# First-layer pieces of two pairs' tails moved later, with a new order and new loads, in a fused windowed-attention and MLP-mixer kernel

## The chip, the cores and the metric

The kernel runs on one core of one Trainium2 chip. The metric is the device time of one execution, in microseconds (us). A core has a matrix engine (PE, with its weight loads shown as PEld), a vector engine (DVE), a scalar engine (ACT), GpSimd (POOL) and SyncE (SP), and DMA engines that move data beside them. POOL and SP do little arithmetic here: POOL issues the loads from memory and some stores, SP issues transposing DMAs (from one on-chip buffer to another) and the other stores.

## What is computed

Eight images of 576 tokens. First, attention over a causal window of 128 tokens, 8 heads of 64 values, with a linear bias per head; then a mixer block with one matrix product pair over tokens and one over channels.

```python
scores = scale * np.matmul(q, k.transpose(0, 1, 3, 2))     # q, k, v: 8 x 8 x 576 x 64
bias = slopes[:, None, None] * (-np.abs(rel))[None, :, :]
mask = (rel >= 0) & (rel < 128)
attn = softmax(np.where(mask, scores + bias[None], -1e9))
x = (attn @ v) as 8 x 576 x 512
h = np.maximum(xt @ w_tok1, 0.0) @ w_tok2                  # over tokens: 576 -> 256 -> 576
u = x + h.transpose(0, 2, 1)
h2 = np.maximum(u @ w_ch1, 0.0) @ w_ch2                    # over channels: 512 -> 1536 -> 512
return u + h2
```

## The kernel before

**Tiling.** An image has 576 tokens: four blocks of 128, called main tokens here, and a tail of 64. Two images (`b` even and odd) form a pair (`pr`); their two tails make one block of 128 rows, `TAIL`, number 8 of the pair's nine blocks. All matrix work is in bf16 with 128 x 128 weights.

**Stages of one image.** `side(b)` does attention and the token mixer: the loaded `qk` blocks are turned (`transposes`; on PE through `ident`, line 679, for the first ten blocks of the run, later by a transposing DMA that SP issues, line 668, from `qk` to `qkT`), then `scores` (PE line 722, exponential on ACT, mask on DVE), `values` (PE line 802, divided into `xb`), then `token_mix` (PE lines 847, 857, 889 and, for the tail, 885), whose result `ub` (tail: `utl`) is turned again by DMA from image 2 on (line 915) into `uT` (tail: `uTt`). `main(b)` does the channel mixer: the first layer writes `r2` (tail: `r2t`), the second layer (`second`, PE line 1326; tail: `tail_second`, PE line 1218) writes the output. While `main(b)` runs, `side(b + 1)` is woven in between.

**The first layer and its pieces.** For the main tokens it consists of twelve chunks (`chunk`, PE line 1085, four matmuls of 512 columns each) or, for a number of images set by `UNITS`, of units (`unit`, PE line 1006) that use seven half-size products instead of eight. `UNITS = [0,0,0,1,2,1,2,3]`: image 3 has one unit and image 7 three. In `main`, images with units run through `for u in range(NHT // 4)`, that is u = 0, 1, 2.

**The tails.** The tails of images 0 to 3 go through the channel mixer together in `main(3)`, those of images 4 to 7 in `main(7)`. The first layer of such a group of tails is done by `tail_piece(t)`: each call makes two pieces of eight matmuls of 256 columns (PE line 1129), each followed by a ReLU on ACT (line 1134) into `r2t`. Three calls, t = 3, 7 and 11, cover the twelve tiles. The pieces read `uTt`, of which the transposing DMA of the group's later pair is the last part.

**What sets the order.** Nothing above runs in the order written. Every call of `plan.op` records an operation with an engine, a cost, a rank (its due time) and its dependences; `Plan.run` then deals the operations out, engine by engine: of those that can start, the one with the smallest start and then the smallest rank. `along` hands out ranks: each operation gets the sum of the costs of those before it in its stage, so the place where a call stands in `main` sets its rank and that of what comes behind it. `SEEDS` shifts the rank of each group of 30 operations within a stage by a pseudo-random amount of up to `SHIFT` = 1500 either way. Loads are the exception: POOL issues them strictly in the order in which they were recorded, for the first pair and the weights that of `LOADS` (`k2` is k of block 2, `W` the token weights, `A` and `B` quarters of the channel weights, `P` and `T` small parts for the tails). Where PE is planned to wait within the first part of the run, `Plan.emit` fills the gap with matmuls on zeros (`spin`, PE line 1418), sized by the gap.

Of the kernel before, what the change touches and what calls it, by code (L numbers as in the profile page):

```python
# [73 lines left out]
class Plan:  # L74
# [235 lines left out]
    def emit(self, spin):  # L310
# [11 lines left out]
        for _, _, go in sorted(work, key=lambda w: w[:2]):  # L322
# [20 lines left out]
RANKH = 0  # L343
RELU = 350
SUMS_AT = 60e3
SEEDS = {0: 517497, 4: 785877, 5: 700536, 6: 16714, 7: 413526, 8: 685397, 10: 382165, 11: 797072, 20: 274424, 21: 252221, 22: 938434, 23: 229954, 30: 618980, 31: 73962, 40: 48116, 41: 463500, 42: 138947, 50: 698411, 60: 77721, 61: 670382, 62: 980070, 70: 272112, 71: 329646, 73: 863296, 80: 860821, 81: 812390, 82: 698755, 90: 642555, 91: 36162, 92: 820492, 100: 378208, 101: 12283, 102: 666882, 110: 374839, 111: 457165, 112: 228977, 122: 958618, 130: 444343, 131: 112543, 132: 417601, 140: 895813, 141: 108506, 142: 904489, 151: 79725, 152: 698131, 153: 848768, 154: 58892}
GROUP = 30
SHIFT = 1500.0
UNIT_LATE = False
# [28 lines left out]
EARLY = 1  # L378


LOADS = ("k2 k8 q2 k1 q1 v3 v0 v1 v8 q8 v2 q7 W1 q5 q6 k6 k7 "
         "W2 v7 v6 k5 A1 q4 A0 k4 B0 A2 v4 A3 B3 B2 v5 P1 T0 B1")


@with_exitstack
def kernel(
# [81 lines left out]
    W1 = const.tile([P, NC, DTOK], BF16, name="W1")  # L468
    W1p = const.tile([P, 2, DTOK], BF16, name="W1p")
    W2 = const.tile([P, NJ, NC * P], BF16, name="W2")  # L470
# [585 lines left out]
    def main(b, rank):  # L1056
# [64 lines left out]
        def tail_piece(t):  # L1121
            uTt = tails_of(pr)[1]
            for w in (t - 3, t - 1):
                cx = bank()

                def gox(w=w, cx=cx):
                    for i in range(2):
                        for cb in range(NCB):
                            pe_.matmul(cx()[:, 2 * i * P : 2 * (i + 1) * P], lhsT=WC1[:, cb, (w + i) * P : (w + i + 1) * P],  # L1129
                                       rhs=uTt()[:, cb, :], start=cb == 0, stop=cb == NCB - 1)  # L1130

                rk = rank(872)
                plan.op("PE", 872, gox, rk, makes=cx, reads=[(uTt, 0), (uTt, 1)], needs=[lc1[w], lc1[w + 1]])
                plan.op("ACT", 600, lambda w=w, cx=cx: act_.activation(
                    out=r2t()[:, w : w + 2, :], in_=cx().rearrange("p (a b) -> p a b", a=2), func=ACT.Relu),
                    rk, part=(r2t, w // 2), uses=[cx], other=("DVE", 690, lambda w=w, cx=cx: dve_.tensor_scalar(
                        out=r2t()[:, w : w + 2, :], in0=cx().rearrange("p (a b) -> p a b", a=2), scalar1=0.0,
                        scalar2=None, op0=ALU.max)))

        if not UNITS[b]:  # L1140
            turn_ = [0, 1, 2, 6, 7, 8, 3, 4, 5, 9, 10, 11] if quick else list(range(NHT))
            for at, t in enumerate(turn_):
                rk = chunk(t)
                if quick and at % 6 == 5:
                    second_sums(at // 6, rk)
                if late_tail and at % 4 == 3:
                    tail_piece(at)
        else:
            tt = halves(b, rank, uT)
            for u in range(NHT // 4):  # L1150
                if u >= NHT // 4 - UNITS[b]:
                    rk = unit(b, u, rank, uT, tt, r2)
                else:
                    for t in (2 * u, 2 * u + 1, 6 + 2 * u, 7 + 2 * u):
                        rk = chunk(t)
                if quick and u:
                    second_sums(u - 1, rk)
                if late_tail:
                    tail_piece(4 * u + 3)
        if late_tail and TAIL_FIRST[pr // 2]:  # L1160
            tail_second(b, rank, r2t)
        second(b, rank, r2, ss, sums, ub)
# [291 lines left out]
```

## Time and profile before

| | us |
|---|---|
| runs | 274.56, 274.52, 273.83 (median 274.52) |
| the profiled execution's own time | 275.12 |
| its span, first to last instruction | 273.4 |
| PE busy | 267.6 |
| DVE busy | 230.4 |
| ACT busy | 148.9 |
| POOL busy (issuing) | 112.9 |

The profile is one execution. Its span leaves out 1.72 us around the program. A busy PE does not mean that PE is at its peak, since a matmul's end is modelled and overlaps the next; how long a stretch took is better read from the starts.

### The profile page before, as it was taken

What the parts mean: (1) busy time and instruction counts of PE and PEld (TensorE: products, weight loads), DVE (VectorE), ACT (ScalarE), POOL (GpSimd) and SP (SyncE); (2) the same over time, 40 slices, a digit from 0 to 9 for tenths busy, and PEclk for the clock granted to TensorE, in tenths of its full rate; (3) what the DMA queues carried; (4) which work ended last, traced back from release to release, by engine and by line L of the source; (5) the groups of instructions that cost most, each with busy time, mean ns of one, the idle gap of its engine ahead of it and who ended that gap; (6) DMA issues with size and microseconds to landing.
All of it is one profiled execution on the core that took longest, in us unless ns stands there. A gap on an engine that the chain in (4) does not pass through costs nothing.

```text
span 273.4 us, 7106 instructions
## 1 busy us (share of the span) xinstructions
PE 267.6 (98%) x2839; PEld 190.0 (69%) x2839; DVE 230.4 (84%) x543; ACT 148.9 (54%) x258; POOL 112.9 (41%) x142
## 2 busy tenths in 40 slices
PE   8999999999999999989999999999999999999994
PEld 4675667575568556765778868586578676888884
DVE  6577799998989499855999979998898899968984
ACT  5384895356931683038951079615960596047720
POOL 8999645950770077500890007800940300040000
PEclk9999999999999999999999999999999999999999
DMA  8999999999998999999999989999996800541016
GB/s 155 154 163 174 192 199 178 153 142 236 148 146 107 179 191 119 141 166 227 116 118 155 223 172 81 139 132 210 178 155 109 217 2 0 79 134 42 1 41 192
DMA packets 167553, 38.71 MB, mean 142 GB/s; under 512 B 155872, under 2 KB 166496, under 8 KB 167520
## 3 DMA queue, kind: packets, MB, share of 16 engines
q0 software_dynamic: 113936, 19.51, 91.7%
q1 hardware_dynamic: 51360, 18.10, 36.2%
q10 hardware_dynamic: 2224, 0.66, 1.2%
q8 instruction: 22, 0.36, 0.6%
q14 instruction: 11, 0.09, 0.1%
HBM read 35.85 MB, written 9.44 MB: 166 GB/s over the span
## 4 chain that ended last, share of the span: by engine, by line
PE 94%; DMA 3%; DVE 1%; issue 0%; DVEq 0%
PE ps L1326 25%; PE ps L1085 19%; PE ps L1006 10%; PE ps L802 7%; PE ps L722 7%; PE ps L847 5%; PE ps L889 4%; PE ps L1418 4%; PE ps L1129 4%; PE ps L1218 3%; DMA uTt<-utl 3%; PE ps L679 2%; PE ps L857 1%; PE ps L885 1%; PE ps L1070 1%; PE ps L924 1%
## 5 line engine op out<-in xcount | busy, mean ns | idle before, releaser
L535 POOL DMA_DIRECT2D v<-in_v_dram x40 | 34.5, 867 | 85.8 <-PE ps L802 84.0
L757 ACT ACTIVATE pe<-ps 128x1024 bf16<-128x1024 f32 (+1 forms) x62 | 56.0, 956 | 19.7 <-PE ps L722 19.5
L1085 PE MATMUL ps<-uT,WC 128*128 128x512 bf16 x232 | 55.4, 380 | 0.0
L1326 PEld LDWEIGHTS <-r 128*128 128x128 bf16 x372 | 35.8, 98 | 6.3 <-issue 0.8
L1091 ACT ACTIVATE r<-ps 128x512 bf16<-128x512 f32 x51 | 29.9, 599 | 18.4 <-PE ps L1085 18.1
L1085 PEld LDWEIGHTS <-WC 128*128 128x128 bf16 x232 | 21.1, 97 | 20.8
L535 POOL DMA_DIRECT2D qk<-in_q_dram x38 | 33.0, 878 | 2.8 <-DMA v<-in_v_dram 2.6
L535 POOL DMA_DIRECT2D qk<-in_k_dram x38 | 33.3, 890 | 1.4 <-DMA WC<-in_moe_w_ch_dram 1.0
L767 DVE TENSOR_TENSOR pe<-pe,mask 128x1024 bf16<-128x1024 bf16 (+1 forms) x50 | 32.4, 664 | 0.9 <-ACT pe L757 0.8
L1326 PEld LDWEIGHTS <-s 128*128 128x128 bf16 x288 | 27.6, 98 | 4.8 <-issue 0.5
L818 DVE TENSOR_TENSOR xb<-ps,rt 128x256 bf16<-128x256 f32 (+1 forms) x68 | 27.3, 416 | 0.7
L802 PEld LDWEIGHTS <-pe 128*128 128x128 bf16 (+1 forms) x560 | 22.4, 98 | 6.1 <-DVE pe L767 1.2
L802 PE MATMUL ps<-v,pe 128*128 128x65 bf16 (+1 forms) x560 | 26.1, 194 | 0.0
L1326 PE MATMUL ps<-WC,r 128*128 128x256 bf16 x192 | 24.4, 273 | 0.0
L1326 PE MATMUL ps<-WT,s 128*128 128x256 bf16 x192 | 23.9, 273 | 0.0
L1326 PE MATMUL ps<-WT,r 128*128 128x256 bf16 x180 | 22.1, 273 | 0.0
L722 PEld LDWEIGHTS <-qkT 64*128 64x128 bf16 x560 | 14.8, 94 | 10.5 <-issue 8.5
L744 ACT ACTIVATE pe<-ps 128x1024 bf16<-128x1024 f32 x7 | 7.2, 1022 | 26.1 <-PE ps L722 26.1
L907 DVE TENSOR_TENSOR ub<-ps,xb 128x512 bf16<-128x512 f32 x30 | 19.0, 683 | 0.8 <-PE ps L889 0.8
L722 PE MATMUL ps<-qkT 64*128 64x128 bf16 (+1 forms) x304 | 19.3, 216 | 0.1
L815 DVE RECIPROCAL rt<-ps 128x4 f32<-128x4 f32 (+1 forms) x76 | 12.6, 176 | 6.0 <-PE ps L802 5.1
L847 PE MATMUL ps<-xb,W 128*128 128x512 bf16 x64 | 16.4, 379 | 0.0
(118 smaller groups left out, 459.4 us busy)
## 6 DMA issues: line engine op xcount, KB each, us to landing
v<-in_v_dram POOLq DMA_DIRECT2D x32, 128.0 KB, 5.3
qk<-in_k_dram POOLq DMA_DIRECT2D x30, 128.0 KB, 5.4
qk<-in_q_dram POOLq DMA_DIRECT2D x30, 128.0 KB, 5.3
WC<-in_moe_w_ch_dram POOLq DMA_DIRECT2D x8, 384.0 KB, 10.0
out_dram<-raw SPq DMA_DIRECT2D x10, 256.0 KB, 2.5
out_dram<-raw SPq DMA_DIRECT2D x18, 128.0 KB, 3.1
out_dram<-ob SPq DMA_DIRECT2D x7, 256.0 KB, 2.5
out_dram<-raw POOLq DMA_DIRECT2D x5, 256.0 KB, 2.6
```

The costliest lines, as they stand in the source:

```text
L535: nc.gpsimd.dma_start(out=to()[p0 : p0 + n, :, :], in_=rows(src, b, s0, n))
L722: pe_.matmul(wide(e)[:, i, 0 if joint else kind, a:z], lhsT=ts[kb]()[e * D : (e + 1) * D, NHP + i, :], rhs=ts[blk]()[e * D : (e + 1) * D, ...
L757: act_.activation(out=pb()[:, e, :, lo:, c0:c1_], in_=wide(e)[:, :, lo:, c0:c1_], func=ACT.Exp, scale=scale)
L767: dve_.tensor_tensor(out=o, in0=o, in1=heads(mk, es), op=ALU.mult)
L802: pe_.matmul(view()[a:z, at, i, :], lhsT=pb()[:, e, i, kind, a:z], rhs=vb()[:, h, 0 : D + 1], start=m == 0, stop=m == len(mms) - 1, skip_g ...
L818: dve_.tensor_tensor(out=x4(), in0=view()[r0:r1_, :, :, 0:D], in1=rt()[r0:r1_, 0:n, :, :].broadcast_to([r1_ - r0, n, 4, D]), op=ALU.mult)
L847: pe_.matmul(t1[j]()[:, :], lhsT=W1[:, c, j * P : (j + 1) * P], rhs=xb()[:, blk, :], start=c == 0, stop=False)
L907: plan.op("DVE", 690, lambda blk=blk, u=u_of(pr, blk)[1], ht=ht, hs=hs: dve_.tensor_tensor(out=u(), in0=ht()[:, hs], in1=xb()[:, blk, :], ...
L1006: pe_.matmul(bk()[:, c * HS : (c + 1) * HS], lhsT=l(c, cb), rhs=r(cb), start=new and c == 0 and cb == 0, stop=cb == 1, skip_group_check=True)
L1085: pe_.matmul(ct()[:, :], lhsT=WC1[:, cb, t * P : (t + 1) * P], rhs=uT()[:, cb, :], start=cb == 0, stop=cb == NCB - 1)
L1091: plan.op("ACT", 600, lambda t=t, ct=ct: act_.activation(out=r2()[:, t, :], in_=ct()[:, :], func=ACT.Relu), rk, part=(r2, t), uses=[ct], o ...
L1326: pe_.matmul(of(bk, c), lhsT=l(t, c), rhs=w(t), start=first, stop=g == 1 and t == HK - 1, skip_group_check=True)
```

## The change

Three things are different, and no arithmetic is.

1. The place of the tail pieces among the main tokens' pieces. Images 3 and 7 both take the path with units. There, `tail_piece(3)`, `(7)` and `(11)` stood behind u = 0, 1 and 2; now nothing stands behind u = 0, `tail_piece(3)` behind u = 1, and `(7)` and `(11)` behind u = 2. The same shift is made in the path without units, which no image with a late tail takes.
2. `SEEDS`, the table that shifts ranks: 47 groups with a number before, 44 now, nearly all with another number.
3. `LOADS`, the order of the first pair's loads and the weights: the same 35 items in another order.

```diff
...
-SEEDS = {0: 517497, 4: 785877, 5: 700536, 6: 16714, 7: 413526, 8: 685397, 10: 382165, 11: 797072, 20: 274424, 21: 252221, 22: 938434, 23: 229954, 30: 618980, 31: 73962, 40: 48116, 41: 463500, 42: 138947, 50: 698411, 60: 77721, 61: 670382, 62: 980070, 70: 272112, 71: 329646, 73: 863296, 80: 860821, 81: 812390, 82: 698755, 90: 642555, 91: 36162, 92: 820492, 100: 378208, 101: 12283, 102: 666882, 110: 374839, 111: 457165, 112: 228977, 122: 958618, 130: 444343, 131: 112543, 132: 417601, 140: 895813, 141: 108506, 142: 904489, 151: 79725, 152: 698131, 153: 848768, 154: 58892}
+SEEDS = {0: 184261, 4: 385444, 6: 691587, 7: 435935, 8: 971243, 10: 14454, 11: 310335, 12: 88060, 20: 451034, 21: 604284, 22: 491458, 23: 654259, 31: 69562, 40: 313502, 41: 516766, 42: 615956, 50: 545906, 51: 396156, 60: 899926, 62: 898557, 70: 192676, 71: 113139, 72: 650006, 73: 567960, 81: 119321, 90: 576549, 92: 820979, 100: 378208, 101: 47453, 102: 655405, 111: 103762, 112: 7071, 121: 349157, 122: 783724, 130: 503198, 132: 893694, 140: 133189, 141: 34590, 142: 311199, 150: 776541, 151: 75250, 152: 65067, 153: 406410, 154: 132943}
...
-LOADS = ("k2 k8 q2 k1 q1 v3 v0 v1 v8 q8 v2 q7 W1 q5 q6 k6 k7 "
-         "W2 v7 v6 k5 A1 q4 A0 k4 B0 A2 v4 A3 B3 B2 v5 P1 T0 B1")
+LOADS = ("k1 k2 q2 q8 v8 q1 k8 v1 v0 W2 k6 v2 v3 W1 k5 q7 q4 "
+         "k7 q5 k4 q6 A0 A2 v7 A3 A1 B2 P1 v4 T0 B0 B1 v6 v5 B3")
...
-                if late_tail and at % 4 == 3:
-                    tail_piece(at)
+                if late_tail and at in (6, 9, 11):
+                    tail_piece({6: 3, 9: 7, 11: 11}[at])
...
-                if late_tail:
-                    tail_piece(4 * u + 3)
+                for t in ([], [3], [7, 11])[u] if late_tail else []:
+                    tail_piece(t)
...
```

How the order comes out is shown at three places. The first is the queue of SP where the tails of images 0 to 3 are turned (`uTt`; `ub1` and `utl0` hold image 3's token-mixer results, `qkT` is turned q and k). Before:

```order
L668 DMA_TRANSPOSE qkT2_79<-qk2_69 128x8x128
L915 DMA_TRANSPOSE uTt0_102<-utl0_95 128x4x128
L915 DMA_TRANSPOSE uT1_101<-ub1_94 128x4x128 x4
L668 DMA_TRANSPOSE qkT1_78<-qk1_68 128x8x128
L1306 DMA out_0_dram<-raw1_107 128x2x256
```

Now:

```order
L668 DMA_TRANSPOSE qkT2_79<-qk3_70 128x8x128
L915 DMA_TRANSPOSE uT1_101<-ub1_94 128x4x128
L915 DMA_TRANSPOSE uTt0_102<-utl0_95 128x4x128
L915 DMA_TRANSPOSE uT1_101<-ub1_94 128x4x128 x3
L668 DMA_TRANSPOSE qkT3_80<-qk2_69 128x8x128
```

One of the four transposing DMAs of image 3's main tokens now stands ahead of that of the tails.

The second is ACT in the same stretch, where every first-layer piece is evicted once, the tails' as line 1134, chunks of main tokens as line 1091 (lines 744 and 757 are the exponentials of scores). Before:

```order
L865 ACTIVATE r110_99<-ps_66 128x512
L744 ACTIVATE pe1_86<-ps_66 128x8x128
L1134 ACTIVATE r2t0_105<-ps_66 128x512 x2
L1091 ACTIVATE r21_104<-ps_66 128x512 x3
L757 ACTIVATE pe0_85<-ps_66 128x1024 x2
L1091 ACTIVATE r21_104<-ps_66 128x512 x2
L757 ACTIVATE pe2_87<-ps_66 128x1024 x2
L1091 ACTIVATE r21_104<-ps_66 128x512 x2
L757 ACTIVATE pe1_86<-ps_66 128x1024 x2
L1134 ACTIVATE r2t0_105<-ps_66 128x512 x2
```

Now:

```order
L1091 ACTIVATE r20_103<-ps_66 128x512
L744 ACTIVATE pe2_87<-ps_66 128x8x128
L1134 ACTIVATE r2t0_105<-ps_66 128x512
L1091 ACTIVATE r21_104<-ps_66 128x512 x2
L757 ACTIVATE pe1_86<-ps_66 128x1024 x2
L1091 ACTIVATE r21_104<-ps_66 128x512 x2
L757 ACTIVATE pe0_85<-ps_66 128x1024 x2
L1091 ACTIVATE r21_104<-ps_66 128x512 x2
L757 ACTIVATE pe2_87<-ps_66 128x1024 x2
L1091 ACTIVATE r21_104<-ps_66 128x512
L1134 ACTIVATE r2t0_105<-ps_66 128x512
```

Of the tails' six pieces in image 3, the second now stands behind seven chunks more, beside the next side's scores (line 757).

The third is POOL, whose loads follow `LOADS`; from the token weights `W1` on (a `qk` buffer takes q and k of one block). Before:

```order
L539 DMA W1_118<-in_moe_w_tok1_dram 128x4x256
L539 DMA W1p_119<-in_moe_w_tok1_dram 64x256
L535 DMA qk4_71<-in_q_dram 128x8x64
L535 DMA qk0_67<-in_q_dram 128x8x64
L535 DMA qk0_67<-in_k_dram 128x8x64
L535 DMA qk3_70<-in_k_dram 128x8x64
L539 DMA W2_120<-in_moe_w_tok2_dram 128x2x512
L535 DMA v1_73<-in_v_dram 128x8x64
L535 DMA v2_74<-in_v_dram 128x8x64
```

Now:

```order
L539 DMA W1_118<-in_moe_w_tok1_dram 128x4x256
L539 DMA W1p_119<-in_moe_w_tok1_dram 64x256
L535 DMA qk4_71<-in_k_dram 128x8x64
L535 DMA qk1_68<-in_q_dram 128x8x64
L535 DMA qk0_67<-in_q_dram 128x8x64
L535 DMA qk1_68<-in_k_dram 128x8x64
L535 DMA qk4_71<-in_q_dram 128x8x64
L535 DMA qk0_67<-in_k_dram 128x8x64
```

Before, PE turned blocks 7 and 6 first of these (`qk3` and `qk0`), complete with the sixth row here. Now it turns blocks 7 and 5 (`qk1` and `qk4`), complete with the sixth and the seventh; `W2`, seventh before, is issued ahead of this stretch now.

## The prediction

> **What bounds the kernel now.** I read the busy times first, then the same times by stage, then what PE waited for, then the chain of waits around the longest wait. In the rows by stage, each engine's busy time is followed by its instructions.
>
> ```profile
> PE 267.6 (98%) x2839; PEld 190.0 (69%) x2839; DVE 230.4 (84%) x543; ACT 148.9 (54%) x258; POOL 112.9 (41%) x142
> ...
> PE   8999999999999999989999999999999999999994
> ...
> PEclk9999999999999999999999999999999999999999
> ...
> 0.00:31.00 31.00, 29.60 (x333) 18.52 (x334) 21.53 (x68) 17.74 (x31) 28.27 (x40) 1.00 1.84 164
> 31.00:117.00 86.00, 85.99 (x916) 55.62 (x915) 75.75 (x177) 47.67 (x81) 44.56 (x54) 1.00 1.71 163
> 117.00:119.00 2.00, 1.08 (x16) 0.76 (x14) 0.82 (x2) 1.02 (x1) 0.00 (x0) 1.00 1.70 74
> 119.00:240.00 121.00, 121.00 (x1304) 88.45 (x1302) 107.52 (x238) 67.68 (x108) 37.62 (x46) 1.00 1.15 138
> 240.00:273.40 33.40, 29.90 (x280) 26.62 (x277) 24.82 (x60) 14.82 (x38) 2.48 (x4) 0.99 0.26 83
> ```
>
> PE is busy 267.6 of 273.4 us at full clock. By stage it is busy 85.99 of 86.00 us from 31 to 117 us and 121.00 of 121.00 us from 119 to 240 us. Only the first 31 us, 2 us in the middle and the last 3.5 us (stores) hold idle time. So the time is PE's own work, plus fillers and waits at the start, plus one wait at 117 us, and an order can gain no more than these.
>
> ```profile
> PE ps L1129 <- DMA uTt<-utl: 0.9, 1, 0.9
> PE ps L924 <- DVE ub L907: 0.3, 1, 0.3
> ...
> 109.05 1.42 PE ps L1326 x12
> 110.47 0.60 PE ps L885 x4
> ...
> 111.09 0.69 DVE utl L907
> ...
> 111.81 6.84 DMA uTt<-utl
> ...
> 118.69 1.03 PE ps L1129 x8
> 119.72 1.31 PE ps L1326 x12
> 121.03 0.24 PE ps L802 x8
> ```
>
> The waits on PE (total us, times, longest) behind its first instruction are two: 0.9 us for the tails' transposing DMA, 0.3 us for `ub` in the start. The chain of waits (start us, us, what) shows the first: the tail's token mixing ends at 110.47 + 0.60 = 111.07, DVE adds until 111.78, the DMA is issued at 111.81 and takes 6.84 us, and PE starts the first tail piece, line 1129, at 118.69.
>
> **What the wait costs.** The idle row is not the whole price, as matmuls overlap.
>
> ```profile
> 117.38 0.40 PE L722 MATMUL ps<-qkT 64*128 64x128 bf16 x8
> 118.69 1.03 PE L1129 MATMUL ps<-uTt,WC 128*128 128x256 bf16 x8 [0.92 <-DMA uTt<-utl]
> ...
> 90.76 1.89 PE L1085 MATMUL ps<-uT,WC 128*128 128x512 bf16 x8
> 92.66 0.23 PE L722 MATMUL ps<-qkT 64*128 64x128 bf16 x2
> ...
> 93.21 1.04 PE L1085 MATMUL ps<-uT,WC 128*128 128x512 bf16 x4
> ```
>
> Sixteen matmuls of line 722 take 0.55 us from first to next start (92.66 to 93.21). One switch of PE between tile shapes (64 rows to 128) is in that: line 1326 x12 took 1.42 us where another shape follows it, and 1.31 where none does, so a switch is 0.11 us, and eight matmuls with a switch take (0.55 - 0.11)/2 + 0.11 = 0.33. From 117.38 PE could have gone on at 117.71 instead of 118.69. The wait costs **0.98 us**.
>
> **The change, part by part.** The matmuls of the real work are the same in number and shape: all 2788. What differs is where they stand, the fillers, the switches and the waits.
>
> *The tail's first piece in image 3.* Between line 885 and the first line 1129, the order of before holds 8 matmuls of line 889, 42 of line 1326 and 8 of line 722; now 4, 60, 8 and also 8 of line 802.
>
> ```profile
> 106.35 1.29 PE ps L847 x6
> ...
> 111.81 1.19 SPq L915 DMA_TRANSPOSE uTt<-utl  x1
> 113.10 5.83 SPq L915 DMA_TRANSPOSE uT<-ub  x4
> ...
> 111.40 1.45 POOL L535 DMA_DIRECT2D qk<-in_k_dram  x2
> ...
> L915 SPq DMA_TRANSPOSE uTt<-utl x3: 1190/1216/1216, 111.8 to 236.0; - x3
> ...
> DMA to landing us min/median/max: 2.4/2.9/6.8
> ```
>
> Line 1326 costs 1.31/12 = 0.109 us each, line 889 has the shape of line 847 (1.29/6 = 0.215), eight of line 802 take 0.24. So PE has 18 x 0.109 - 4 x 0.215 + 0.24 = 1.34 us more to do first. The DMA came 118.65 - 111.07 = 7.58 us after line 885; PE was ready after 7.62 - 0.98 = 6.64, and now after 7.98. Against that, `uTt` now stands second in SP's queue behind one `uT`, and SP takes 113.10 - 111.81 = 1.29 us from one issue to the next. The block of that `uT` is finished two of line 889 and line 885 itself ahead of the tail's, 0.43 + 0.60 = 1.03 us, so `uTt` is issued 0.26 us later: 7.84. POOL's loads, which were still being issued until 112.85 (111.40 + 1.45), are freed by values at the same distance ahead of line 885 as before, so they lie on the DMA as they did. The margin is 0.14 us. The ends are -0.98 (gone) and +0.26 (the later issue, were the 1.34 us of work eaten elsewhere). I take **-0.9**, near the end of the counted rows.
>
> A rule weighed here: the row says 2.4, 2.9 and 6.8 us to landing for the three `uTt` DMAs. The Trainium skill (DMA: Bandwidth & Descriptors, Anatomy of one DMA) gives, fitted for DMAs that GpSimd issues, 2.0 us plus bytes/436e3; for 128 KB that is an estimate of 2.3 us. The trace agrees for two, not for the one at 111.81, beside POOL's loads. By the rule the DMA would not be what PE waited for, and this term would be 0, not -0.9; that is a rival below.
>
> *Pieces moved on.* The second piece of image 3 goes behind seven chunks, and the last one stays 1.75 us of PE work (12 + 4 matmuls) ahead of `tail_second` in both kernels. Their ReLUs on ACT move with them. ACT is busy 148.9 of 273.4 us, and that covers it: 0. In image 7 the first piece comes earlier: 8 of line 889, 4 of line 1006 (the shape of line 1326) and 30 of line 1326 behind line 885, 1.73 + 34 x 0.109 = 5.4 us.
>
> ```profile
> 236.02 1.22 SPq L915 DMA_TRANSPOSE uTt<-utl  x1
> ```
>
> There `uTt` stood behind two `uT`; now it is first. With utl 0.9 us behind line 885 and 2.4 to 2.9 us to landing it is there after 3.8: no wait, 1.6 us to spare.
>
> *Fillers.* 51 with 21,800 columns before, 52 with 22,704 now, all before image 0's first layer.
>
> ```profile
> 14.81 1.47 PE L1418 MATMUL ps<-zero 128*128 128x512 bf16 x6
> 16.21 0.23 PE L722 MATMUL ps<-qkT 64*128 64x128 bf16 x2
> ```
>
> Six of 512 columns ran from 14.81 to 16.21, less a switch of 0.11: 0.42 ns a column. 904 more cost **+0.38 us**, unless what they cover arrives earlier than the filler ends; they can't be negative.
>
> *Switches.* PE changes shape 98 times before, 96 times now: -2 x 0.11 = **-0.2**.
>
> *Loads.* All loads are issued as before, in another order, the same sum on POOL. At the block turned second by line 679, after the first token mixing, the order is tightest.
>
> ```profile
> 24.10 1.07 PE L679 MATMUL ps<-ident,qk 128*128 128x128 bf16 x16
> 25.00 0.60 PE L889 MATMUL ps<-r,W 128*128 128x512 bf16 x2
> ...
> 17.06 1.87 POOL L535 DMA_DIRECT2D qk<-in_k_dram  x2
> ...
> 19.49 1.92 POOL L535 DMA_DIRECT2D v<-in_v_dram  x2
> ...
> DMA to landing us min/median/max: 4.7/5.9/11.6
> ...
> L535 POOL DMA_DIRECT2D v<-in_v_dram x40 | 34.5, 867 | 85.8 <-PE ps L802 84.0 <-DMA WC<-in_moe_w_ch_dram 1.0 <-DMA qk<-in_k_dram 0.4
> ```
>
> Before, the blocks turned there, 7 and 6, were complete with k7, issued as the second of the two k loads at 17.06 (about 18), and PE came at 24.10. Now the second block is 5 and needs q5, two DMAs on, the place of the first v load at 19.49. PE comes there later by the block ahead of it, (25.00 - 24.10)/2 = 0.45 us, and by about 0.6 us of fillers and what they pushed back: 25.15. With 4.7 to 5.9 us to landing (minimum and median of the early v loads) q5 is there at 24.2 to 25.4. The wait is 0 to 0.3; a slot missed costs 0.87 us, the price of one load on POOL. I take **+0.2**, ends 0 and +0.87. The old wait of 0.3 us for `ub` (line 924) has its cause gone, as the block that came last there now goes to ACT instead of DVE, with 20 matmuls of line 679's kind, 1.1 us, ahead of its use: **-0.3**, ends -0.3 and +0.3 (DVE late again).
>
> *Scores behind the transposes of image 2.* SP issues four `uT`, then the first `qkT` of the next side.
>
> ```profile
> 82.56 5.12 SPq L915 DMA_TRANSPOSE uT<-ub  x4
> 87.78 2.63 SPq L668 DMA_TRANSPOSE qkT<-qk  x2
> ...
> qkT<-qk SPq DMA_TRANSPOSE x26, 3.9
> ```
>
> Before, PE reached that `qkT` (line 722, at 92.66) almost as it landed: eight chunk matmuls at 0.215 from 90.76 and a switch end at 92.59, so it waited 0.07 us. Now there are 66 of line 1326, 8 chunk matmuls and 4 of line 802 between, not 60, 12 and 8: 6 x 0.109 - 4 x 0.215 - 0.12 = 0.33 us less. If the DMA, 4.8 us from 87.78, is as slow again, PE waits 0.40; if it is as quick as the 3.9 us of its kind's median, not at all. I take **+0.3**, ends 0 and +0.4.
>
> **The sum.** -0.9 + 0.38 - 0.2 + 0.2 - 0.3 + 0.3 = -0.5 us. The profiled execution took 275.12, so it would take 274.6; it lies 0.6 above the median of the runs, so against the median: **274.0 us**. A difference below 0.3% (0.82 us) is about what a measurement of this kernel can't tell from none. What is late next: after 119 us nothing on PE waited, and behind 150 us the two orders are within 0.1 us of PE work of one another, so no new wait is counted there.
>
> **The rivals.**
>
> *All at the good ends.* The wait goes, the `qkT` DMA is quick, q5 is there: -0.98 + 0.38 - 0.2 - 0.3 = -1.1, 273.4 us. For it: PE has no other wait to lose. Against it: three tight places must all hold. Chance 0.24.
>
> *The wait isn't the DMA's length, or the second place in the queue eats the shift.* Then the term is 0 and the sum +0.4, 274.9 us; the change would not do what its first part is about. For it: the margin of 0.14 us. Against it: 6.84 us in the chain. Chance 0.12.
>
> *Slower: the first 30 us lose load slots.* `W2` and two v blocks now come ahead of blocks that PE turns; each slot missed at line 679 or 847 is 0.87 us for the whole of PE, which has no slack later to make it good. From two slots on it decides: -0.5 - 0.2 + 1.74 = +1.0, 275.5 us; three give 276.4. For it: the DMA engines are the limit there and the place has 0 to 0.3 us. Against it: the slots were counted by rows. Other waits that no row of before shows would look alike. Chance 0.24.
>
> **How the numbers follow.** The forecast has 0.40, with its own range 273.4 to 274.7 (the wait kept to a third, the `qkT` and q5 terms at either end). Faster by over 0.3%, below 273.7: the good ends 0.24 and 0.10 of the forecast's, 0.34. Slower, above 275.34: the load slots' 0.24 less a little under the bound, and a little of the second rival, 0.24. Between: 0.42. The range for 8 in 10 is 273.0 to 275.9, from the good ends to the middle of the slower case.
>
> **What would show it.** Right: in the waits on PE, no row for `uTt` at line 1129, or one of up to 0.3; line 1418 at 52 instructions; PE idle in the first 31 us like the 1.4 us here. The `qkT` step: a PEld row for line 722 and a DMA of 0.3 to 0.5 near 92 us. Wrong: PE's first line 1085 or 1070 later than about 31 us (the slots), a `uTt` row of about 0.9 (the second rival), or PE idle between 120 and 240 us, which nothing here foresees.

## Result and profile after

The changed kernel takes **274.97 us** (median of 11 executions, 274.27 to 275.47), the kernel before 274.35 (273.83 to 274.63): a ratio of 1.0029, 95% interval 1.0021 to 1.0038. It is slower by 0.6 us where 0.5 less was forecast. The time lies inside the range given.

Busy times of the changed kernel's profiled execution (275.40 us):

```profile
span 273.3 us, 7116 instructions
...
PE 267.4 (98%) x2840; PEld 190.2 (70%) x2840; DVE 229.4 (84%) x542; ACT 148.4 (54%) x256; POOL 113.0 (41%) x142
```

The same by stage, with the columns as in the prediction:

```profile
0.00:31.00 31.00, 28.78 (x320) 17.98 (x320) 20.96 (x64) 15.25 (x28) 27.39 (x39) 1.00 1.81 164
31.00:117.00 86.00, 86.00 (x930) 55.24 (x927) 74.94 (x181) 50.56 (x82) 45.39 (x55) 1.00 1.79 166
117.00:119.00 2.00, 2.00 (x27) 1.82 (x25) 1.63 (x3) 0.00 (x0) 0.00 (x0) 1.00 0.66 55
119.00:240.00 121.00, 121.00 (x1298) 88.73 (x1296) 106.55 (x237) 68.53 (x110) 38.05 (x46) 1.00 1.13 136
```

The wait at 117 us is gone (2.00 of 2.00 busy). The first 31 us have lost: 28.78 busy in place of 29.60. The waits on PE (total us, times, longest) say where:

```profile
PE ps L679 <- DMA qk<-in_k_dram: 0.8, 1, 0.8
PE ps L679 <- DMA qk<-in_q_dram: 0.3, 1, 0.3
```

PE's timeline shows the place (start us, us, what, in brackets the idle time ahead of it):

```profile
24.70 0.40 PE L679 MATMUL ps<-ident,qk 128*128 128x128 bf16 x4
25.90 0.40 PE L679 MATMUL ps<-ident,qk 128*128 128x128 bf16 x4 [0.80 <-DMA qk<-in_k_dram]
26.60 0.62 PE L679 MATMUL ps<-ident,qk 128*128 128x128 bf16 x8 [0.31 <-DMA qk<-in_q_dram]
```

PE turns blocks 7 and 5 there, and k7, then q5, come too late. From start to start the two waits cost 0.97 and 0.48 us beyond the matmuls' own time. The chain of waits tells the same. Until 26.6 us it runs along POOL's issues of loads, and only then along PE (first rows and the change-over):

```profile
1.37 6.87 DMA qk<-in_k_dram
8.53 0.69 POOL qk L535
...
17.57 2.29 POOL qk L535 x3
20.18 6.38 DMA qk<-in_q_dram
26.60 0.62 PE ps L679 x8
27.23 0.86 PE ps L889 x4
```

That shows a start bound by loads, but not why the kernel is slower: the waits that are gone, 0.98 us at 117 us and 0.45 us for `ub` at line 924 (both from start to start), were worth as much as the two new ones, 1.45 us. In the two profiled executions PE's last matmul even starts earlier in the changed kernel (269.37 us) than before (269.68). So either these two executions aren't typical, or the loss lies behind that matmul, and the experiments begin with that.

### The profile page after: what moved, and what is told of

The parts are those of the page before. It is cut to its first block, busy times and chain, and to the rows that moved or that the text cites. A ratio compares the mean times of both kernels' runs of the same rounds, so it can differ in the third digit from the quotient of the medians.

```text
span 273.3 us, 7116 instructions
## 1 busy us (share of the span) xinstructions
PE 267.4 (98%) x2840; PEld 190.2 (70%) x2840; DVE 229.4 (84%) x542; ACT 148.4 (54%) x256; POOL 113.0 (41%) x142
## 4 chain that ended last, share of the span: by engine, by line
PE 88%; DMA 5%; POOL 4%; issue 1%; DVE 1%; DVEq 0%; POOLq 0%
PE ps L1326 26%; PE ps L1085 19%; PE ps L1006 10%; PE ps L802 6%; PE ps L722 6%; PE ps L889 5%; PE ps L847 5%; PE ps L1129 4%; PE ps L1218 3%; DMA qk<-in_k_dram 3%; DMA qk<-in_q_dram 2%; POOL qk L535 2%; PE ps L857 1%; POOL v L535 1%; PE ps L885 1%
## 5 line engine op out<-in xcount | busy, mean ns | idle before, releaser
L1085 PE MATMUL ps<-uT,WC 128*128 128x512 bf16 x232 | 56.0, 379 | 0.0
L802 PE MATMUL ps<-v,pe 128*128 128x65 bf16 (+1 forms) x560 | 25.3, 194 | 0.0
L1326 PE MATMUL ps<-WC,r 128*128 128x256 bf16 x192 | 25.1, 273 | 0.0
L1326 PE MATMUL ps<-WT,s 128*128 128x256 bf16 x192 | 24.6, 273 | 0.0
L815 DVE RECIPROCAL rt<-ps 128x4 f32<-128x4 f32 (+1 forms) x76 | 11.7, 173 | 6.8 <-PE ps L802 6.3
L1306 POOL DMA_DIRECT2D out_dram<-raw x5 | 3.6, 714 | 33.2 <-issue 21.8
```

The source lines that it names most:

```text
L802: pe_.matmul(view()[a:z, at, i, :], lhsT=pb()[:, e, i, kind, a:z], rhs=vb()[:, h, 0 : D + 1], start=m == 0, stop=m == len(mms) - 1, skip_g ...
L1085: pe_.matmul(ct()[:, :], lhsT=WC1[:, cb, t * P : (t + 1) * P], rhs=uT()[:, cb, :], start=cb == 0, stop=cb == NCB - 1)
L1326: pe_.matmul(of(bk, c), lhsT=l(t, c), rhs=w(t), start=first, stop=g == 1 and t == HK - 1, skip_group_check=True)
```

## Experiments

Of each kernel a time (median, ratio to the kernel before on the same chip), and of each timed execution the span. "Outside" below is the mean of time less span. In the edits, `behind` is a helper put between planning and writing out: it takes the finished order and moves one load of POOL's behind another. Where an edit sets `t0`, the planned start, it moves one instruction on its engine in the same way. The rest of the order stays.

The first two groups ask whether the wait at 117 us is the kernel's, the next three what the late loads and the end cost, the last what the parts of the change do alone.

### Both kernels again

No edit.

> The kernel before, unchanged, taken again. What it tells: its spans beside its times, and whether its trace shows the same waits a second time. The load theory (the change removes 0.98 us at line 1129 and loses about 1.45 us at line 679): the same wait of 0.9 us for uTt at line 1129 and no wait at line 679; time equal to the kernel before within 0.1%. The rival that the uTt wait belongs to the one profiled execution (its 275.12 us lay 0.6 above the median of the runs): no uTt row here, or one below 0.3 us, and spans near 272.4 us. The rival that the loss lies outside the span: time less span 1.7 here, 2.07 for the changed kernel.

> The changed kernel, unchanged, taken again. Load theory: ratio 1.002 to 1.004 again; waits at line 679 for a k and a q load, together 0.8 to 1.2 us in the rows, no row for uTt. The theory that the second widening of the loads' landing times (the last of a load's 16 completions 2.3 us behind the first from 23.6 us on, as the second fetch of instructions runs on the same DMA engine as the first) is an accident of one execution: here the last completion of k7 is 1.5 us behind the first, k7 lands near 25.0 instead of 25.85, and the two waits are 0.3 us in all.

Measured: before 274.04 us, 0.9994 (0.9985 to 1.0003); after 275.04 us, 1.0026 (1.0014 to 1.0038). The waits on PE of the kernel before, taken again:

```profile
PE ps L1418 <- DVE zero L499: 1.0, 1, 1.0
PE ps L924 <- DVE ub L907: 0.3, 1, 0.3
```

Its row by stage at 117 us:

```profile
117.00:119.00 2.00, 2.00 (x24) 1.54 (x23) 0.84 (x2) 1.21 (x2) 0.00 (x0) 1.00 0.35 67
```

PE's timeline at the place:

```profile
117.36 0.40 PE L722 MATMUL ps<-qkT 64*128 64x128 bf16 x8
117.68 1.05 PE L1129 MATMUL ps<-uTt,WC 128*128 128x256 bf16 x8
```

There is no wait for `uTt`. SP issued the DMA at 111.79 us, as in the execution that the prediction read (111.81), and PE began the piece at 117.68, when it got there. The DMA's semaphore counts 16 completions. Here are the first and the last three, with the fetch of instructions (16 KB each, a queue of their own) that ran nearby:

```
                    first   ...      last three           fetch: start, length
before              116.46       117.03  117.05  118.65    116.59  1.27
before, again       115.71       116.20  116.22  116.27    116.04  1.38
```

In the execution that was read, 15 parts were there at 117.05, and one came 1.6 us behind. A fetch was running from 116.59 to 117.86 us; on which DMA engine the trace doesn't say. That it held the sixteenth part is possible, not shown: a fetch ran beside the same DMA in the second execution too, and no part was late. Shown is that the wait isn't the kernel's. None of the four other traces below whose edits leave this place alone (three memsets more, twice; four memsets on POOL; four loads on SP) has a row for `uTt`. The median span of 134 executions of the kernel before, over all groups, is 272.3 us, and only 9 of them reach 273.2. The profiled one had 273.4, and 0.98 less is 272.4.

In the spans of these two groups the change costs 0.5 us (mean 272.45 of the executions of before that stood beside, 272.97 of the changed kernel taken again). Outside the span it costs 0.25 more (1.77 and 2.02). Of the two waits at line 679 that for k7 is there again (0.84 us from start to start), that for q5 is not, and others have come at line 802. So k7's late landing was no accident of the first execution: it was complete at 25.85 us there and at 25.77 here. The waits on PE, changed kernel taken again:

```profile
PE ps L679 <- DMA qk<-in_k_dram: 0.7, 1, 0.7
PE ps L802 <- DMA v<-in_v_dram: 0.6, 2, 0.3
```

### The first tail piece alone, later

```diff
+    piece = [o for o in plan.ops if o.part == 7 and o.emit.__qualname__.endswith("tail_piece.<locals>.gox")][0]
+    relu = [o for o in plan.ops if o.part == 7 and o.n == piece.n + 1][0]
+    piece.t0, relu.t0 = 119480.0, 120400.0
+    [x for x in piece.bufs if x.ring is plan.rings["ps"]][0].slot = (2,)
```

> The kernel before with one part of the change alone: the first tail piece of image 3 (8 matmuls of line 1129 and the ReLU behind them) stands behind 12 matmuls of line 1326 and 8 of line 802, 1.55 us of PE work later, in another PSUM bank; order and loads are else those of before. My reading of the wait: no uTt row, the stretch from 117 to 119 us busy throughout, the span shorter by 0.98 us and the time too: 273.4 us, a ratio of 0.9965. The rival that the wait is an accident of the profiled execution: no uTt row, but the time equal to the kernel before within 0.1%. The rival that a freed PE waits at the next place: a new row behind 119 us of up to 0.98 and no gain.

Measured: 274.62 us, 1.0019 (1.0008 to 1.0029): slower. PE's timeline at the place:

```profile
117.08 0.40 PE L722 MATMUL ps<-qkT 64*128 64x128 bf16 x8
117.93 1.47 PE L1326 MATMUL ps<-WT,r 128*128 128x256 bf16 x12 [0.45 <-DVE raw L1289]
119.33 0.42 PE L802 MATMUL ps<-v,pe 128*128 128x65 bf16 x8
119.58 1.58 PE L1129 MATMUL ps<-uTt,WC 128*128 128x256 bf16 x13
```

DVE's timeline there:

```profile
117.19 0.69 DVE L1289 TENSOR_TENSOR raw<-ps,raw 128x512 f32<-128x512 f32 x1 [0.62 <-PE ps L1326]
```

In the order of before the piece stood between line 722 and twelve matmuls of line 1326 that need a PSUM bank which DVE empties until 117.88. The piece was the cover for that. With it gone, PE waits at line 1326: eight matmuls of line 722 take 0.85 us from start to the next start, 0.32 in the kernel before. From the first line 885 to the first line 1358 this trace takes 0.62 us longer than the kernel before, taken again. The spans agree, as all 12 are 272.7 or more. So the move by itself gains nothing where `uTt` is in time, and it loses its cover. The changed kernel's order, drawn up as a whole, has no such wait there.

### One load behind

```diff
+    behind("q4", "q5")
```

> The changed kernel with one load moved: q4, which PE needs only with k4 at about 29.9 us, is issued two places later, behind q5, so k7 and q5 come one place (0.87 us of POOL) earlier. Nothing else on any engine moves. Load theory: the waits at line 679 shrink from 1.1 us in the rows to 0.2 or less, and the time falls by 0.8 to 0.9 us, to 274.1 or a ratio of 0.999 to the kernel before. Rivals (the loss lies at the end of the kernel, outside the span, or in the moved pieces): the waits shrink, but the time stays within 0.2 us of the changed kernel, a ratio of 1.002 to 1.003.

Measured: 274.78 us, 1.0022 (1.0011 to 1.0033). In its profile the waits at line 679 are gone, as expected, PE's last matmul starts 0.84 us earlier than in the changed kernel (268.53), and the span is 272.4. But over twelve executions the span's mean falls only by 0.28, to 272.69, and the 0.8 to 0.9 expected of the time isn't there. Part of the profile's gain belongs to its execution, in which the parts of each load landed closer together than in the two of the changed kernel (last section). Its waits say what is late next:

```profile
PE ps L802 <- DMA v<-in_v_dram: 0.4, 1, 0.4
```

To see this in several executions I read when lines are first reached. In the changed order, PE goes from the first line 885 (image 1's tail) to the first line 1358 (the last stage) in 211.95 us, in each of the nine traces of that order here, to 0.01; in the order of before it is 213.4, except where one of the waits near 117 us stands in it. So up to the last stage, all that differs between kernels of the changed order happens before line 885. The two orders have different work ahead of that line: as 211.95 + 55.5 = 213.42 + 54.0, the changed order is level with the kernel before at line 1358 when it gets to line 885 at 55.5 us.

```
start of the first        L889   L1326   L885   |  v5 landed
before, again             25.00  44.15   54.00  |  44.06
after                     27.06  43.94   56.15  |  45.57
after, again              26.59  43.87   56.33  |  46.06
one load behind (q4)      25.41  42.86   55.31  |  45.05
```

The second late place is the last `v` block, v5. In the changed `LOADS` it stands behind the weights B0 and B1, and PE needs it at line 802 near 45 us. Taken again, the changed kernel was 0.5 us quicker than the first time at line 889, but v5 came at 46.06, and it was 0.2 later at line 885.

### Nothing but the end, and the instruction counts

The idle instructions near the end of DVE: five memsets that stood behind the last add of line 1289 before stand ahead of it now. Timeline of DVE, the kernel before:

```profile
268.61 0.69 DVE L1289 TENSOR_TENSOR raw<-ps,raw 128x512 f32<-128x512 f32 x1
269.26 0.59 DVE L1410 MEMSET zero<- 128x1 bf16 x5
```

The changed kernel (the row of its fifth memset, at 268.81, is left out):

```profile
268.29 0.45 DVE L1410 MEMSET zero<- 128x1 bf16 x4
268.78 0.69 DVE L1289 TENSOR_TENSOR raw<-ps,raw 128x512 f32<-128x512 f32 x1
```

From the start of PE's last matmul to the end of the span it is 3.68 us before and 3.89 after. The first kernel here puts the memsets back behind the add; the second takes three memsets out of the changed kernel, the third puts three into the kernel before. The last two look for the 0.25 us outside the span: in the traces, an 8 KB fetch of instructions stands 1.9 us behind the span in the changed kernel, and in none of before.

```diff
+    idle = max((o for o in plan.ops if o.eng == "DVE" and o.rank > 5e8), key=lambda o: o.t0)
+    idle.t0 = min(o.t0 for o in plan.ops if o.eng == "DVE" and o.t0 > idle.t0) + 1
...
-            ("DVE", 5, 60, 266.5e3, lambda: dve_.memset(zero[:, 1:2], 0.0))):
+            ("DVE", 2, 150, 266.5e3, lambda: dve_.memset(zero[:, 1:2], 0.0))):
...
+                [dve_.memset(W1p[(1 - i) * R : (2 - i) * R, i, :], 0.0) for _ in range(4 - 3 * i)]
```

> The changed kernel with DVE's second group of idle memsets behind the last add of line 1289 in place of ahead of it, as in the kernel before; still 640 instructions. Theory of the end (from PE's last matmul to the span's end is 3.88 us in the changed kernel and 3.68 before, as the memsets hold that add and the stores behind it): 3.68 here, span 0.2 us shorter, time less span 2.02 still, ratio 1.002. Rival (the stores' landing sets the end whatever DVE does): 3.9 us, no gain.

> The changed kernel with three idle memsets fewer in the first of DVE's two groups near its end: 637 instructions on DVE. Theory of the last fetch: no fetch behind the span, time less span falls from 2.02 to about 1.77. As the second group of memsets then starts 0.35 us earlier, the last add of line 1289 behind it is up to 0.35 us earlier too, and the span up to 0.2 shorter: together 274.5 to 274.7, a ratio near 1.0015. Rival (neither matters): 1.0026 as before.

> The kernel before with three more memsets on DVE near 4 us, where DVE waits for the first inputs; this makes 640 instructions on DVE, as the changed kernel has, in place of 637. Theory of the last fetch (the changed kernel's traces show one more 8 KB fetch of instructions at about 275 us, 1.9 us behind the span's end, which those of before lack; 640 is five blocks of 128): such a fetch shows here too, and time less span rises from 1.77 to about 2.05, span unchanged at 272.3 to 272.5: a ratio of 1.001. Rival (the time outside the span hangs on the order of loads or stores): time less span stays 1.77 and no fetch behind the span.

Measured: 274.62 us, 1.0020 (1.0009 to 1.0032) with the memsets behind; 274.74 us, 1.0025 (1.0014 to 1.0037) with three fewer; 273.55 us, 0.9987 (0.9975 to 0.9999) with three more in the kernel before. The first came out as expected: 3.68 us from the last matmul, span 0.2 shorter (mean 272.76), outside still 1.97. So the memsets' place costs **0.2 us**. The other two refute the count of DVE's instructions: with 637 the fetch behind the span is still there and outside is 1.99, with 640 there is none and outside is 1.78.

The gain of the third wasn't expected, so it was taken again.

> The kernel before with three more memsets on DVE near 4 us, taken again, as it came out 0.0013 faster than the kernel before (0.9975 to 0.9999) against my expectation. If that is the order of the first 30 us (its trace has no wait at line 924 and 0.28 us less at the first line 722, 0.6 us together): again 0.998 to 0.999 and first line 1085 near 29.25 us in place of 29.87. If it was chance: 1.000, and 29.87.

Measured: 273.89 us, 0.9984 (0.9974 to 0.9995). So this kernel is faster than both, by about 0.4 us. Its two traces have no wait at line 924, and line 1085 starts at 29.25 and 29.61 us. Why three memsets at 4 us do that isn't shown; DVE's copy behind line 924, which came 0.9 us behind PE's start there in the kernel before, comes 0.5 behind it in these two.

### All loads in time

First, four edits at once:

```diff
+    behind("q4", "q5")
+    behind("B2", "v4")
...
+    idle.t0 = min(o.t0 for o in plan.ops if o.eng == "DVE" and o.t0 > idle.t0) + 1
...
-            ("DVE", 5, 60, 266.5e3, lambda: dve_.memset(zero[:, 1:2], 0.0))):
+            ("DVE", 2, 150, 266.5e3, lambda: dve_.memset(zero[:, 1:2], 0.0))):
```

> The changed kernel with q4 behind q5, the load B2 behind v4 (PE waited 0.4 to 0.57 us at line 802 for v4 near 39 us; B2 is needed from 44 us on), the three memsets fewer, and the second group of memsets behind the last add. If the four terms stand for themselves: -0.26 (q4, measured), -0.3 to -0.5 (v4), -0.27 (last fetch), -0.2 (the end), from 275.0: 273.8 to 274.0, a ratio of 0.999, as fast as the kernel before or faster. Rival (a PE that is freed waits at the next late load): no row for v at line 802 near 39 us but new ones near 45 us, and a ratio of 1.001 or more.

Measured: 274.83 us, 1.0020 (1.0011 to 1.0029). The 273.8 to 274.0 us that the four terms added up to aren't met. The rival holds, though its waits are the old ones: v6 and v5, longer (the waits at line 679 are down to 0.4 us). PE stood at line 1326 1.1 us earlier than in the changed kernel (42.83), and at line 885 no earlier (56.25). PE's timeline:

```profile
44.35 0.29 PE L802 MATMUL ps<-v,pe 128*128 128x65 bf16 x4
45.19 0.53 PE L802 MATMUL ps<-v,pe 128*128 128x65 bf16 x12 [0.56 <-DMA v<-in_v_dram]
46.04 0.42 PE L802 MATMUL ps<-v,pe 128*128 128x65 bf16 x8 [0.32 <-DMA v<-in_v_dram]
```

v6 landed at 45.15 and v5 at 45.99, and PE went on at 45.19 and 46.04. Next, v6 and v5 go ahead of the weights B1. In the first kernel that is the only load that moves, in the second the loads of the four edits move too. Both have the memsets behind the add, and the second also has four idle copies fewer on ACT:

```diff
+    behind("B1", "v5")
```

> The changed kernel with the memsets behind the last add (as measured: span 0.2 us shorter) and one load moved: B1, 0.4 MB of weights, issued behind v6 and v5 in place of ahead of them, so that v6 and v5 land 1.9 us earlier. Floor theory (in the changed order PE can't leave line 802 near 45 us before v5 has landed, at 45.05 to 46.06 us in six traces, and has a fixed amount of work from there: 211.95 us from the first line 885 to the first line 1358 in all six): alone this takes away only what v5 cost, as PE still waits at line 679 near 25 us: first line 885 at 55.6 to 55.8 in place of 55.3 to 56.3, the time 0 to 0.3 us below the kernel with the memsets alone (274.62): 274.3 to 274.6, ratio 1.001 to 1.002. Rival (v5 isn't a floor): no change, or a loss where the weights come too late at line 1326 near 46 us.

> The changed kernel with q4 behind q5, B2 behind v4, B1 behind v6 and v5, the memsets behind the last add, and four idle copies fewer on ACT (354 instructions there, as in the kernel before, in place of 358). Floor theory: with the waits at line 679 and line 802 all shortened, PE reaches the first line 885 at 54.9 to 55.2 us (56.25 with the first three edits alone, 56.15 and 56.33 in the changed kernel), and the span is 271.8 to 272.2. Time less span tells of ACT: 1.77 if the 0.25 us outside the span come of ACT's instruction count, else 2.0. Together 273.6 to 274.2, ratio 0.998 to 1.000, no slower than the kernel before. Rival (a freed PE waits at the next late load, whichever it is): first line 885 at 55.8 or later, ratio 1.001 or more.

Measured: the one load 274.55 us, 1.0028 (1.0010 to 1.0046), first line 885 at 55.46; with the other loads 275.03 us, 1.0039 (1.0024 to 1.0053), first line 885 at 56.03, not the 54.9 to 55.2 expected. In the second no load is waited for on PE any more, and it is no faster. The wait has gone to DVE. Waits on PE of that kernel:

```profile
PE ps L802 <- DVE xb L818: 1.0, 1, 1.0
```

Its timeline of DVE:

```profile
43.25 0.55 DVE L596 TENSOR_TENSOR WT<-WC 128x768 bf16<-128x768 bf16 x1
45.26 0.56 DVE L596 TENSOR_TENSOR WT<-WC 128x768 bf16<-128x768 bf16 x1 [1.46 <-DMA WC<-in_moe_w_ch_dram]
45.74 0.55 DVE L596 TENSOR_TENSOR WT<-WC,WT 128x768 bf16<-128x768 bf16 x1
46.20 0.31 DVE L815 RECIPROCAL rt<-ps 128x4 f32<-128x4 f32 x3
46.43 0.73 DVE L818 TENSOR_TENSOR xb<-ps,rt 128x256 bf16<-128x256 f32 x2
```

A sum of weights (line 596) stands in DVE's queue for B1, which landed at 45.24, and behind it the divisions that free PE's banks. The last kernel moves that sum behind the divisions too:

```diff
+    sums = [o for o in plan.ops if o.emit.__qualname__.endswith("weight_sums.<locals>.go")]
+    sums[4].t0 = 46200.0
```

> The changed kernel with q4 behind q5, B2 behind v4, B1 behind v6 and v5, the memsets behind the last add, and one weight sum of DVE (the first of the second group, line 596, which reads B1) behind the token mixing's divisions of line 818 in place of ahead of them. In the kernel without this last edit DVE stood 1.46 us at that sum, and PE 1.03 us at line 802 behind it. Floor theory (each wait of the first 50 us is a late load, seen by PE or by an engine that PE waits for; with all of them out of the way PE has nothing to wait for): first line 885 at 54.8 to 55.2 us (56.03 without the last edit), span 271.8 to 272.1, and with 2.0 us outside the span 273.8 to 274.1: a ratio of 0.999 to 1.000. Rival (another load or engine is late in its place): first line 885 at 55.8 or later, a ratio of 1.002 or more.

Measured: 274.53 us, 1.0001 (0.9987 to 1.0014). Its profile is as expected: line 885 at 55.05 us, span 271.9, and one row is left of the waits on PE, the one for its first weights:

```profile
PE ps L1418 <- DVE zero L499: 1.0, 1, 1.0
```

The mean span is 272.42, 0.55 below the changed kernel's (0.2 of it the memsets) and level with that of before (272.56 beside it). It isn't always as in its profile: the twelve spans run from 271.7 to 272.8, and the 273.8 to 274.1 us expected aren't met. With 2.01 us outside the span the time is that of the kernel before.

### One part of the change alone, and what lies outside the span

Three kernels with one part (or two) of the change each; the planner draws up the rest anew. Two more add idle instructions to the kernel before: four memsets on POOL behind its loads, and four small loads, which nobody reads, at SP's start.

```diff
+    for _ in range(4):
+        nc.gpsimd.memset(zero[:, 5:6], 0.0)
...
+    for i in range(4):
+        nc.sync.dma_start(out=spare[i : i + 1, :], in_=k[0, 0, i : i + 1, :])
```

> The kernel before with the new places of the tail's pieces alone; order and loads are drawn up by the planner from the tables of before, so other instructions move too. If the places are worth the 0.98 us of my prediction: faster than before, 0.997. If the wait for uTt is in few executions: the places give nothing, and what the planner moves beside them costs what it costs, ratio 1.000 to 1.006. SP has 203 instructions, POOL 222: time less span near 1.77 if SP's count (206 in the changed kernel) is behind the 2.0.

> The kernel before with the new order of loads alone, the rest drawn up from the tables of before. Load theory: waits for late loads at lines 679 and 802 ahead of the first line 885, span 272.7 to 274, ratio 1.002 to 1.006. Rival (the loads' order costs nothing): no such rows, 1.000. Time less span (SP has 206 instructions): 2.0 if SP's count or the loads' order is behind it, 1.77 if neither.

> The changed kernel with the loads of before: new places and new table of the order, old order of loads. Load theory: the waits at line 679 for k7 and q5 and those at line 802 for v5 and v6 are absent or others, as this order was drawn up for other loads; ratio 0.999 to 1.004. Time less span (SP has 206 instructions, POOL 221): 2.0 if SP's count or the order is behind it, 1.77 if the loads' order is.

> The kernel before with four memsets on POOL behind all of its loads: 225 instructions there, as in the changed kernel's copies (224 or 225), in place of 221. If POOL's count sets the 0.25 us outside the span and the fetch of instructions behind it: a fetch at about 274 us and time less span 2.0, ratio 1.001. Else no fetch, 1.77, ratio 1.000.

> The kernel before with four small loads (256 bytes each) more in SP's queue at its start, where SP is idle; nobody reads them. SP has 208 instructions then in place of 202 (the changed kernel 206, the kernel with the new places alone 203, and 1.80 us outside the span). If SP's count sets what lies outside the span: time less span 2.0 and a fetch of instructions about 1.9 us behind the span's end, ratio 1.001. Else 1.77 and no fetch. The span is to stay within 0.2 us of 272.4.

Measured: new places alone about 306 us, 1.1157 (1.1115 to 1.1199); new loads alone 281.93, 1.0284 (1.0255 to 1.0312); places and table without the loads 279.73, 1.0195 (1.0170 to 1.0220); four on POOL 274.01, 0.9998 (0.9986 to 1.0009); four on SP 274.36, 1.0011 (0.9997 to 1.0024). None of the first three came out as expected. The three parts are one: the table of the order fits one list of loads and one set of places, and each part alone makes the planner's order so much worse that these runs don't price the part. With the places alone the granted clock was lower besides, 0.97 in the profiled execution. Its two largest waits on PE (at 196 and 266 us):

```profile
PE ps L1085 <- DMA uT<-ub: 7.4, 2, 5.7
PE ps L1129 <- DMA uTt<-utl: 4.3, 1, 4.3
```

My load theory foresaw waits at lines 679 and 802 with the new loads alone; there were none for loads there, the largest was 2.3 us at line 1085 for `uT`.

Outside the span: 1.79 with four more on POOL and no fetch behind the span, so POOL's count is out, as DVE's and (in the kernel with v5 first, 354 on ACT, 2.07) ACT's. With four more loads on SP (208 instructions) the fetch is there, 1.6 us behind the span, and outside is 1.88, which is 0.11 above the kernel before beside it. With the places alone (203 on SP) there is no fetch, and outside is 1.79; with 206 it is 1.95 (the new loads alone) and 2.04 (places and table).

But SP's count does not decide it alone. The fetch is absent from two traces with 206 instructions on SP, that of the four edits and that of the new loads alone, and these two executions have 1.77 and 1.76 us outside. In all 19 traces fetch and time go together: the nine without the fetch have 1.76 to 1.80 us outside, the ten with it 1.92 to 2.15. And the changed kernel's own executions, taken again, range from 1.74 to 2.18, where no execution of the kernel before is above 1.84. So the fetch was seen only with 206 or 208 instructions on SP, and not in every execution then. That it makes the delay isn't shown, and why the mean is 0.25 in the changed kernel and 0.11 with the four loads stays open.

## Why the prediction was wrong

**The tail's first piece, "I take -0.9".** This is the step that failed. The row was read rightly (0.98 us, one DMA of 6.84 us), but it belonged to one execution, not to the kernel: it is in the trace that was read and in none of the five others that have the piece at that place. The sign was in the numbers shown. The profiled execution took 275.12 us, above all three timed ones, and the prediction took its distance to the median, 0.6 us, off at the end without asking which row of the profile was that distance. It was this row, so most of its time was taken off twice.

Without the term my sum is +0.4, 274.9 us, which is the rival given 0.12. That this lies beside the measured 274.97 is luck, as is the time's place inside the range: the terms below were off in both directions, and the 0.45 us found at the end and outside the span stood in none of them. The rival's other half, that the second place in SP's queue eats the shift, did not happen: in the changed kernel `uTt` was complete at 116.84 us, and PE began the piece at 118.63. One wait that the prediction had no word for was hidden under the old place in the order of before, that of line 1326 for DVE.

The rule weighed there points the right way. The estimate of 2.3 us worked out from the Trainium skill (DMA: Bandwidth & Descriptors, Anatomy of one DMA) puts the DMA well ahead of PE, and the term at 0. Taken again, the DMA was issued at 111.79 and its last part came at 116.27, so it took 4.5 us: the conclusion is met, the figure isn't. The Trainium skill, in the section of the same title on why a DMA increments its semaphore by 16, says that up to 16 engines finish independently; the trace agrees, with one part of sixteen 1.6 us behind the others.

**Loads, "+0.2".** The line was right, the block and the size wrong. The prediction looked at the second block alone, through q5. But 0.97 of the 1.45 us in the first profile, and all of the 0.84 in the second, is the wait for k7, in the first block. k7 stands one place later than before and was issued 1.39 us later (17.92 and 19.31 us), as `W2`, k5 and q4 are ahead of it now, and q5 and q6 no longer. Its first part landed at 23.44, its last at 25.85, and PE was there at 24.93. q5 was issued at 20.18, not at the 19.49 that the prediction took, and landed 6.38 us later, not 4.7 to 5.9. So PE's wait isn't a price per lost slot but the lateness of whichever load is last. And line 679 is not the only place: v6, v5 and B1 near 45 us are as tight, which the prediction didn't look for, since PE had no wait there before. The slower rival ("the first 30 us lose load slots", 0.24) names the mechanism; its two slots at 0.87 are 1.74, and its place ends 15 us too early.

**Fillers, "+0.38", and switches, "-0.2".** The fillers are 52, as counted. They can't be added to waits for loads: where the chain runs along POOL until 26.6 us, PE that gets there earlier waits longer. The runs don't price either term apart.

**The `ub` wait, "-0.3".** Right: no row at line 924 in any trace of the changed order, 0.45 us from start to start before. **The scores behind image 2's transposes, "+0.3".** Not there: no row for `qkT` in the waits. The DMA issued at 87.72 us was complete at 90.76, after 3.0 us and not 4.8, and PE came at 92.40. **Pieces moved on, 0.** Nothing against it: from 119 to 240 us PE is busy 121.00 of 121.00 us in the changed kernel too.

**What no step had.** The memsets ahead of the last add (+0.2, shown by putting them back), and 0.25 us outside the span, which goes with a late fetch of instructions and whose cause is open. So the measured 0.6 to 0.9 us are about 0.2 at the end, 0.25 outside the span, and about 0.3 in the first 50 us. The last figure is what is left of the 0.5 in the spans. That it is the late loads, which take more than the `ub` wait gives, is shown by the kernel with all of them out of the way: its spans are level with the kernel before.

## What to carry to other kernels

A wait in one profiled execution is a term only if the execution stands where the timed ones do: when it lies above them, look first which row makes up the distance, and take that row out of the sum. In a start where the chain of waits runs along the queue of loads, an edit is priced by when each load is needed and lands, down to the last one, since a PE freed at one load waits at the next, or behind another engine that stands for it. An instruction that seems to wait may also be another's cover: before moving it, ask what ran beside it.

## What the runs showed of the hardware

The 16 completions of one load lie 0.4 to 1.1 us apart at the start of a run and further apart later, in steps, and much of a step stays. Width in us from first to last completion, by the load's place in POOL's queue, counted from 0:

```
place in the queue        4     11    15    21    29    36
before                   0.50  0.63  1.51  1.49  1.46  1.49
after                    0.79  1.49  1.27  2.41  2.42  2.29
after, again             0.50  1.31  1.72  2.35  2.81  2.84
one load behind (q4)     0.57  1.26  1.44  1.59  1.85  1.93
```

Many steps fall where a fetch of 16 KB of instructions is running. In the changed kernel one runs at 13.45 us (1.19 long) and one at 23.60 (0.94 long), and k7, place 21, has its first completion at 23.44 and its last at 25.85. The first fetch, at 13.4 to 15.1 us, goes with a wider load at place 11 or 12 in all 16 traces of the two orders. Later ones needn't: in the kernel before, those at 23.15 and 35.29 us leave the width as it is. While the queue is full, a part that has fallen behind mostly stays behind (taken again, the changed kernel won back 0.5 us at place 22), and every later load is complete that much later.

The size differs from execution to execution: 1.4 to 2.9 us at place 36 in the nine traces of the changed order, 1.2 to 1.6 in the seven of the order of before. The difference is as much as the waits of the changed order, so its late loads are late by their place in the queue and by this spread together. That the fetch makes the step was not tried.
